# Layer 2 of a two-layer f32 feed-forward kernel: its second block's x asked 8 tiles ahead, its planner given other durations, its last three tiles in another order

## The chip, the core and the metric

One core of one Trainium2 chip runs the whole program. The metric is the device time of one execution in microseconds (us); three runs of the kernel before are given, and one more execution was taken with the hardware profiler.

## What is computed

Linear attention over 8 batches of 8 heads (softmax of q over the head, of k over the sequence, k transposed times v, q times that) gives x of 4608 tokens by 512. Two feed-forward layers follow, each 512 to 2048 to 512, in f32:

```
h = x @ moe_w_in;   g = where(h > 0, h, exp(min(h, 0)) - 1);   x1 = g @ moe_w_out
h = x1 @ moe2_w_in
P = a[0] + a[1]*h + a[2]*h*h + a[3]*h*h*h
Q = 1 + abs(b[0])*abs(h) + abs(b[1])*h*h
out = (P / (Q + 1e-6)) @ moe2_w_out
```

## The kernel before

**Tiles.** A layer has 9 blocks of 512 tokens (j) and 16 slices of 128 of the 2048 inner columns (f). One (layer, j, f) is a tile. Its *in* part, `plan_in`, makes h of 128 x 512 in one PSUM bank (name `ps`, kind `bank`, 4 of them) with 12 matmuls: 4 pieces of x times 3, since each f32 operand is split into a high and a low half of the type that the matmul takes (L781 to L783 hold the three products). Its *out* part, `plan_out`, adds g times w_out into the four accumulators of the block (`acc`), 12 matmuls again (L823). For f = 0 and f = 15 both parts are four operations of 3 matmuls, else one of 12. Layer 2 is 144 tiles of 24 matmuls.

**Between the two parts of a tile of layer 2** stand eleven elementwise operations of 128 x 512, in `plan_rational`: on ACT `pstart` (a[3]*h + a[2], tile `p`, L926), `square` (`s`, L922) and `absb` (|b0 h|, tile `m`, L918), which read the bank; on DVE `pmul` and `pstep` (L944, L947), which read the bank too, the second of them setting it free; on POOL `qsum` (L929); on ACT `root` and `guess` (L932, L935); on DVE `test`, `newton`, `pend` (L938, L941, L951), of which each reads two SBUF tiles; on ACT `hi` and on POOL `lo` (the high and low half of g, L299 and L302; tile `gs` for even f, `g` for odd f). `p` has 3 buffers, and `lo` sets one free; g has 4 in all.

**Order.** All instructions of an engine run in the order in which a planner in the program (`Plan.run`) issues them. It goes through operations with a price each (the number in `ACT(0.8)`, `DVE(0.7)` and so on), takes the one that by these prices can start first, and breaks ties by rank. A price is thus never a time on the chip; it sets only what stands behind what on an engine. PE's order, too, comes out of it.

**x of layer 2.** `plan_x1` loads a block's four pieces of x1 (SP), and makes the high half on ACT and the low half on POOL, with ranks that start 14 tiles ahead of the block, 2 tiles apart.

**Stores.** `plan_store` copies a finished accumulator to `e` on ACT (L863) and sends it off from SP (L867).

Of the kernel before, what the change touches and what calls it, by code (L numbers as in the profile page):

```python
# [13 lines left out]
AF = mybir.ActivationFunctionType  # L14
ALU = mybir.AluOpType
# [19 lines left out]
class Plan:  # L35
# [146 lines left out]
def linear_attention_elu_rational(  # L182
# [46 lines left out]
    late = []  # L229
# [18 lines left out]
    op = plan.op  # L248
# [19 lines left out]
    NTL = 2 * NB * KF
    DMA = 2.2

    def f32_tile(tag, bufs, pool=None):
        return (pool or main).tile([P, TB], F32, tag=tag, name=tag, bufs=bufs)
# [19 lines left out]
    def halves_of(ap):  # L292
        return ap.rearrange("p (h c) -> p h c", h=2)

    def back(ps):
        return ps.rearrange("p (c h) -> p h c", h=2)

    def copy_hi(hi, src):
        nc.scalar.activation(out=hi, in_=src, func=AF.Copy)  # L299
# [454 lines left out]
    in_ops = {}  # L754
# [7 lines left out]
    tiles = [(0, j, f) for part in range(2) for j in range(2) for f in range(*((0, CUT[j]), (CUT[j], KF))[part])]  # L762
# [3 lines left out]
    def step_of(L, j, f):  # L766
        return place[L, j, f]
# [75 lines left out]
    accs = {}  # L843
# [6 lines left out]
    def plan_store(L, j, i, o, r, half):  # L850
        b = {}

        def load(e):
            b["e"] = f32_tile("e", 4)
            nc.sync.dma_start(out=b["e"], in_=part_d[j, i])

        def add(e):
            e = halves_of(b["e"])
            nc.vector.tensor_tensor(out=e, in0=e, in1=back(accs[L, j, i]), op=ALU.add)

        def copy(e):
            b["e"] = f32_tile("e", 4)
            nc.scalar.activation(out=halves_of(b["e"]), in_=back(accs[L, j, i]), func=AF.Copy)  # L863

        def store(e):
            dst = part_d[j, i] if half == 1 else x1_d[j, i] if L == 0 else out[j * TB + i * P:j * TB + (i + 1) * P, :]
            nc.sync.dma_start(out=dst, in_=b["e"])  # L867

        free = [("acc", acc_op[L, j, i])]
        if half == 2:  # L870
            l = op(SP, load, [parts_stored[j, i], in_ops[0, j, KF - 1]], r - 1, take=["e"], extra=DMA)
            o1 = op(DVE(), add, [l, o], r, free=free)
        else:
            l = o1 = op(ACT(), copy, [o], r, take=["e"], free=free)
        o = op(SP, store, [o1], r, extra=DMA, free=[("e", l)])
        if half == 1:
            parts_stored[j, i] = o
        else:
            stored[L, j, i] = o
# [31 lines left out]
    def plan_rational(t):  # L911
        b = {}
        s = step_of(*t)
        gkind = ("gs", "g2")[t[2] % 2]

        def absb(e):
            b["a"] = f32_tile("m", 2)
            nc.scalar.activation(out=b["a"], in_=b["h"], func=AF.Abs, scale=b_sb[:, 0:1])  # L918

        def square(e):  # L920
            b["s"] = f32_tile("s", 3, late[0])
            nc.scalar.activation(out=b["s"], in_=b["h"], func=AF.Square, scale=b_sb[:, 1:2])  # L922

        def pstart(e):
            b["p"] = f32_tile("p", 3, late[0])
            nc.scalar.activation(out=b["p"], in_=b["h"], func=AF.Identity, scale=a_sb[:, 3:4], bias=a_sb[:, 2:3])  # L926

        def qsum(e):
            engine[e].tensor_tensor(out=b["s"], in0=b["s"], in1=b["a"], op=ALU.add)  # L929

        def root(e):
            nc.scalar.activation(out=b["a"], in_=b["s"], func=AF.Abs_reciprocal_sqrt, scale=2.0**-48, bias=qbias)  # L932

        def guess(e):
            nc.scalar.activation(out=b["a"], in_=b["a"], func=AF.Square, scale=2.0**-24)  # L935

        def test(e):
            nc.vector.scalar_tensor_tensor(out=b["s"], in0=b["s"], scalar=1.0 + 1e-6, in1=b["a"], op0=ALU.add, op1=ALU.mult)  # L938

        def newton(e):  # L940
            nc.vector.scalar_tensor_tensor(out=b["a"], in0=b["s"], scalar=-2.0, in1=b["a"], op0=ALU.add, op1=ALU.mult)  # L941

        def pmul(e):
            nc.vector.tensor_tensor(out=b["p"], in0=b["p"], in1=b["h"], op=ALU.mult)  # L944

        def pstep(e):
            nc.vector.scalar_tensor_tensor(out=b["p"], in0=b["p"], scalar=a_sb[:, 1:2], in1=b["h"],  # L947
                                           op0=ALU.add, op1=ALU.mult)

        def pend(e):  # L950
            nc.vector.scalar_tensor_tensor(out=b["p"], in0=b["p"], scalar=a_sb[:, 0:1], in1=b["a"],  # L951
                                           op0=ALU.add, op1=ALU.mult)

        def hi(e):
            if gkind == "gs":
                b["g"] = main.tile([P, 2, TB], F32R, tag="gs", name="gs", bufs=2)
            else:
                b["g"] = late[0].tile([P, 2, TB], F32R, tag="g2", name="g2", bufs=2)
            copy_hi(b["g"][:, 0], b["p"])

        def lo(e):
            sub_lo(e, b["g"][:, 1], b["p"], b["g"][:, 0])

        o = plan_in(t, b)
        p1 = op(ACT(0.8), pstart, [o, late_op], s + 0.5, take=["p"])
        o1 = op(ACT(0.69), square, [p1], s + 0.52, take=["s"])
        o2 = op(ACT(0.69), absb, [o1], s + 0.53, take=["m"])
        p2 = op(DVE(0.7), pmul, [p1], s + 0.6)
        p3 = op(DVE(0.7), pstep, [p2, o2], s + 0.61, free=[("bank", b["h_op"])])
        o3 = op(SOONEST if s >= NTL - 2 else POOL(), qsum, [o2], s + 0.7)  # L970
        o4 = op(ACT(0.72), root, [o3], s + 0.8)
        o5 = op(ACT(), guess, [o4], s + 0.82)
        o6 = op(DVE(1.0), test, [o5], s + 0.9)
        o7 = op(DVE(1.0), newton, [o6], s + 0.91, free=[("s", o1)])
        p4 = op(DVE(1.0), pend, [o7, p3], s + 1.01, free=[("m", o2)])
        g1 = op(ACT(), hi, [p4], s + 1.3, take=[gkind])
        b["g_op"] = op(SOONEST if s >= NTL - 2 else POOL(), lo, [g1], s + 1.4, free=[("p", p1)])
        b["g_free"] = (gkind, g1)
        plan_out(t, b)

# [20 lines left out]
    for n in range(2 * KF):  # L1001
        f, which = divmod(n, 2)
        s = KF + 3 * n
# [7 lines left out]
    late_op = op((("", 0.0),), open_late, at_ops, None)  # L1011

    for f in range(KF):
        for which in range(2):
            b = {}
            r = step_of(0, NB - 1, f) + (0.9, 3.0)[which]
# [7 lines left out]
            l = op(SP, load, [late_op, stored["w", f, which], gone], r, take=["hc"], extra=DMA)  # L1024
# [14 lines left out]
    def plan_x1(j, i):  # L1039
        b = {}  # L1040
        kind = "xs"
        r = step_of(1, j, 0) - 14 + 2 * i

        def load(e):
            b["e"] = f32_tile("e", 4)
            nc.sync.dma_start(out=b["e"], in_=x1_d[j, i])
            x_tile[1, j, i] = main.tile([P, 2, TB], F32R, tag="xs", name="xs", bufs=8)

        def hi(e):
            copy_hi(x_tile[1, j, i][:, 0], b["e"])  # L1050

        def lo(e):
            x = x_tile[1, j, i]
            sub_lo(e, x[:, 1], b["e"], x[:, 0])

        early = in_ops[tiles[max(0, step_of(1, j, 0) - 14)]]
        l = op(SP, load, [late_op, stored[0, j, i], early, last.get("x1")], r, take=["e", kind], extra=DMA)
        last["x1"] = l
        o = op(ACT(), hi, [l], r + 1)
        x_ready[1, j, i] = op(POOL(), lo, [o], r + 1.1, free=[("e", l)])  # L1060
        x_owner[1, j, i] = kind, l
# [7 lines left out]
    with tc.manual_schedule():  # L1069
# [25 lines left out]
        o = op(SP, load_ab, [in_ops[0, 1, 0]], 0.0)  # L1095
        op(ACT(0.2), minus_a, [o, in_ops[0, 2, 0]], 0.0)
        o = op(ACT(0.2), abs_b1, [o, in_ops[0, 2, 0]], 0.0)
        o = op(DVE(0.1), seed_b1, [o], 0.0)
        for _ in range(3):
            o = op(DVE(0.5), heron, [o], 0.0)  # L1100
# [69 lines left out]
```

## Time and profile before

| what | value |
|---|---|
| three runs | 1587.16, 1588.49 (median), 1590.0 us |
| the profiled execution: own time | 1586.46 us |
| its span, first to last instruction | 1584.7 us |
| busy share: PE, DVE, ACT, POOL | 99%, 67%, 66%, 46% |
| granted TensorE clock, mean | 0.999 of full speed |

In the profile PE is TensorE's matmuls, DVE VectorE, ACT ScalarE, POOL GpSimd, SP the engine that issues the DMAs. A time in brackets behind an instruction is how long its engine had stood idle before it, and what ended that. In names, what is written stands left of `<-`, and numbers of buffers are left out.

### The profile page before, as it was taken

The numbers are of one execution on the slowest core, as the hardware profiler recorded it, in microseconds if no ns is written. First come the engines' busy times: TensorE is split into PE (matmuls) and PEld (weight loads), VectorE is DVE, ScalarE is ACT, GpSimd is POOL, SyncE is SP. The second block draws the span as 40 slices with busy tenths as digits, with TensorE's granted clock in tenths as the row PEclk, the third lists the DMA queues.
The fourth block names the chain that finished last, engine by engine and source line by source line (L and its number), as shares of the span: only waits on it lengthen the run. The fifth ranks groups of instructions, "written<-read, shape, count | busy, mean of one in ns | idle before, by whom it ended". The sixth has DMA issues, their size and how long they took to land.

```text
span 1584.7 us, 22781 instructions
## 1 busy us (share of the span) xinstructions
PE 1566.1 (99%) x8344; PEld 1350.2 (85%) x8344; DVE 1056.1 (67%) x1659; ACT 1038.9 (66%) x1825; POOL 727.4 (46%) x529
## 2 busy tenths in 40 slices
PE   8999999999999999999999999999999999999998
PEld 7788888888888888888887888888888888888886
DVE  7998766564656566431227867786877686778776
ACT  6767655554646455444558777777777777777776
POOL 3201223232333232333666666666566657665554
PEclk9999999999999999999999999999999999999999
DMA  9523542332322332101422010101010100100000
GB/s 352 202 85 98 170 145 96 98 117 77 123 92 90 103 114 85 50 5 44 137 87 80 0 54 1 54 1 54 1 53 1 42 13 21 34 7 21 0 28 27
DMA packets 48784, 113.31 MB, mean 72 GB/s; under 512 B 5664, under 2 KB 5664, under 8 KB 46624
## 3 DMA queue, kind: packets, MB, share of 16 engines
q1 hardware_dynamic: 48672, 111.85, 20.6%
q8 instruction: 66, 1.08, 0.3%
q14 instruction: 46, 0.38, 0.1%
HBM read 82.47 MB, written 29.36 MB: 71 GB/s over the span
## 4 chain that ended last, share of the span: by engine, by line
PE 91%; ACT 3%; DVE 2%; issue 2%; POOL 1%; DMA 0%; POOLq 0%; SPq 0%; DVEq 0%; ACTq 0%
PE acc L823 44%; PE ps L781 15%; PE ps L783 15%; PE ps L782 15%; PE ps L637 1%; PE ps L510 1%; ACT p L926 1%; POOL gs L302 1%; ACT s L922 1%; ACT m L932 0%; ACT m L935 0%; DMA e<-in_q_dram 0%; DVE s L938 0%; PE ps L276 0%; DVE m L941 0%
## 5 line engine op out<-in xcount | busy, mean ns | idle before, releaser
L781 PE MATMUL ps<-xs,w_in 128*128 128x512 f32 x1152 | 437.7, 380 | 3.3 <-DVE p L947 3.0
L782 PE MATMUL ps<-xs,w_in 128*128 128x512 f32 x1152 | 436.7, 379 | 0.0
L783 PE MATMUL ps<-xs,w_in 128*128 128x512 f32 x1152 | 436.6, 379 | 0.0
L823 PE MATMUL acc<-gs,w_out 128*128 128x512 f32 x1728 | 403.5, 381 | 2.0 <-DVE w_out L302 1.5
L823 PEld LDWEIGHTS acc<-gs,w_out 128*128 128x128 f32 x1728 | 324.2, 189 | 54.0 <-ACT gs L299 3.5
L302 POOL TENSOR_TENSOR gs<-m,gs 128x512 fp32r<-128x512 f32 x96 | 124.6, 1298 | 283.8 <-ACT gs L299 266.0
L781 PEld LDWEIGHTS ps<-xs,w_in 128*128 128x128 f32 x1152 | 217.7, 189 | 36.7 <-issue 4.4
L782 PEld LDWEIGHTS ps<-xs,w_in 128*128 128x128 f32 x1152 | 217.7, 189 | 30.9 <-DVE xs L302 0.2
L783 PEld LDWEIGHTS ps<-xs,w_in 128*128 128x128 f32 x1152 | 217.7, 189 | 30.8
L893 DVE SCALAR_TENSOR_TENSOR m<-m,ps 128x512 f32<-128x512 f32 x144 | 98.4, 683 | 196.1 <-ACT m L890 189.0
L929 POOL TENSOR_TENSOR s<-s,m 128x512 f32<-128x512 f32 x144 | 218.5, 1518 | 16.9 <-ACT m L918 16.9
L302 POOL TENSOR_TENSOR gs<-p,gs 128x512 fp32r<-128x512 f32 x72 | 116.0, 1611 | 231.9 <-issue 193.5
L823 PE MATMUL acc<-w_out,gs 128*128 128x512 f32 x864 | 201.8, 380 | 2.7 <-ACT gs L299 1.6
L823 PE MATMUL acc<-w_out,g 128*128 128x512 f32 x864 | 199.8, 379 | 0.5 <-POOL g L302 0.5
L887 ACT ACTIVATE m<-ps 128x512 f32<-128x512 f32 x144 | 85.9, 597 | 161.5 <-PE ps L783 128.6
L938 DVE SCALAR_TENSOR_TENSOR s<-s,m 128x512 f32<-128x512 f32 x144 | 142.5, 990 | 69.1 <-ACT m L935 69.0
L823 PEld LDWEIGHTS acc<-w_out,gs 128*128 128x128 f32 x864 | 162.4, 189 | 29.0 <-POOL gs L302 4.3
L823 PEld LDWEIGHTS acc<-w_out,g 128*128 128x128 f32 x864 | 163.2, 189 | 24.0 <-POOL g L302 0.9
L926 ACT ACTIVATE p<-ps,a_sb 128x512 f32<-128x512 f32 x144 | 112.2, 779 | 79.7 <-POOL gs L302 73.6
L299 ACT ACTIVATE gs<-m 128x512 fp32r<-128x512 f32 x144 | 90.4, 628 | 99.0 <-PE acc L823 80.5
L947 DVE SCALAR_TENSOR_TENSOR p<-p,a_sb,ps 128x512 f32<-128x512 f32 x144 | 107.4, 746 | 57.4 <-ACT m L918 57.3
L951 DVE SCALAR_TENSOR_TENSOR p<-p,a_sb,m 128x512 f32<-128x512 f32 x144 | 136.7, 949 | 2.1
(122 smaller groups left out, 1922.5 us busy)
## 6 DMA issues: line engine op xcount, KB each, us to landing
x<-e SPq DMA_DIRECT2D x36, 256.0 KB, 2.2
e<-x SPq DMA_DIRECT2D x36, 256.0 KB, 3.0
out_dram<-e SPq DMA_DIRECT2D x36, 256.0 KB, 2.0
bits<-in_moe_w_in_dram SPq DMA_DIRECT2D x8, 1024.0 KB, 9.6
bits<-in_moe_w_out_dram SPq DMA_DIRECT2D x8, 1024.0 KB, 11.4
st<-in_moe_w_in_dram SPq DMA_DIRECT2D x16, 512.0 KB, 4.6
w<-st SPq DMA_DIRECT2D x32, 256.0 KB, 2.0
st<-in_moe_w_out_dram SPq DMA_DIRECT2D x16, 512.0 KB, 4.2
```

Of the source, the lines that this page charges most:

```text
L299: nc.scalar.activation(out=hi, in_=src, func=AF.Copy)
L302: engine[e].tensor_tensor(out=lo, in0=src, in1=hi.bitcast(F32), op=ALU.subtract)
L781: nc.tensor.matmul(o, w[:, 0, kk, :], two(x[:, 0]), start=(kk == 0), stop=False)
L782: nc.tensor.matmul(o, w[:, 0, kk, :], two(x[:, 1]), start=False, stop=False)
L783: nc.tensor.matmul(o, w[:, 1, kk, :], two(x[:, 0]), start=False, stop=(kk == KD - 1))
L823: nc.tensor.matmul(turned(o), lhsT, two(rhs), start=(f == f0 and n == 0), stop=(f == f1 and n == 2))
L893: nc.vector.scalar_tensor_tensor(out=b["m"], in0=b["m"], scalar=-1.0, in1=b["h"], op0=ALU.add, op1=ALU.max)
L926: nc.scalar.activation(out=b["p"], in_=b["h"], func=AF.Identity, scale=a_sb[:, 3:4], bias=a_sb[:, 2:3])
L929: engine[e].tensor_tensor(out=b["s"], in0=b["s"], in1=b["a"], op=ALU.add)
L938: nc.vector.scalar_tensor_tensor(out=b["s"], in0=b["s"], scalar=1.0 + 1e-6, in1=b["a"], op0=ALU.add, op1=ALU.mult)
L947: nc.vector.scalar_tensor_tensor(out=b["p"], in0=b["p"], scalar=a_sb[:, 1:2], in1=b["h"], op0=ALU.add, op1=ALU.mult)
L951: nc.vector.scalar_tensor_tensor(out=b["p"], in0=b["p"], scalar=a_sb[:, 0:1], in1=b["a"], op0=ALU.add, op1=ALU.mult)
```

## The change

It moves x of layer 2's second block from 14 to 8 tiles ahead; it gives the planner other prices for layer 2's eleven operations; in the last three tiles `square` and `absb` come ahead of `pstart`, |h| lies in a buffer of kind `e`, and in the last two p lies in one of kind `hc` (free by then) and `lo` is fixed to DVE; and the last accumulator's copy is shared by ACT and DVE.

```diff
@@ plan_store
-            nc.scalar.activation(out=halves_of(b["e"]), in_=back(accs[L, j, i]), func=AF.Copy)
+            half = slice(0, 1 if (L, j, i) == (1, NB - 1, 3) else 2)
+            nc.scalar.activation(out=halves_of(b["e"])[:, half], in_=back(accs[L, j, i])[:, half], func=AF.Copy)
+
+        def rest(e):
+            nc.vector.tensor_scalar(out=halves_of(b["e"])[:, 1], in0=back(accs[L, j, i])[:, 1], scalar1=1.0, scalar2=None,
+                                    op0=ALU.mult)
...
+            if shared:
+                o1 = op(DVE(0.4), rest, [l], r, free=free)
@@ plan_rational
+        ending = s >= NTL - 3
+        akind = "e" if ending else "m"
+        pkind = "hc" if s >= NTL - 2 else "p"
...
-        p1 = op(ACT(0.8), pstart, [o, late_op], s + 0.5, take=["p"])
-        o1 = op(ACT(0.69), square, [p1], s + 0.52, take=["s"])
-        o2 = op(ACT(0.69), absb, [o1], s + 0.53, take=["m"])
-        p2 = op(DVE(0.7), pmul, [p1], s + 0.6)
-        p3 = op(DVE(0.7), pstep, [p2, o2], s + 0.61, free=[("bank", b["h_op"])])
...
+        if ending:
+            o1 = op(ACT(0.61), square, [o], s + 0.5, take=["s"])
+            o2 = op(ACT(0.61), absb, [o1], s + 0.51, take=[akind])
+            p1 = op(ACT(0.72), pstart, [o2], s + 0.53, take=[pkind])
+        else:
+            p1 = op(ACT(0.72), pstart, [o, late_op], s + 0.5, take=["p"])
+            o1 = op(ACT(0.61), square, [p1], s + 0.52, take=["s"])
+            o2 = op(ACT(0.61), absb, [o1], s + 0.53, take=["m"])
+        p2 = op(DVE(0.62), pmul, [p1], s + 0.6)
+        p3 = op(DVE(0.68), pstep, [p2, o2], s + 0.61, free=[("bank", b["h_op"])])
+        o3 = op(SOONEST if s >= NTL - 2 else POOL(1.45), qsum, [o2], s + 0.7)
...
-        b["g_op"] = op(SOONEST if s >= NTL - 2 else POOL(), lo, [g1], s + 1.4, free=[("p", p1)])
+        b["g_op"] = op(DVE(0.7) if s >= NTL - 2 else POOL(1.45), lo, [g1], s + 1.4, free=[(pkind, p1)])
@@ plan_x1
-        r = step_of(1, j, 0) - 14 + 2 * i
+        ahead = 14 if j != 1 else 8
+        r = step_of(1, j, 0) - ahead + 2 * i
```

**POOL, first block of layer 2.** Here `s<-s,m` is `qsum`, `gs` and `g2` the `lo` of an even and an odd tile, and `xs` a piece of the second block's x. Before:

```order
L929 TENSOR_TENSOR s_7761<-s_7761,m_7782 128x512
L302 TENSOR_TENSOR g2_7794<-p_7673,g2_7794 128x512
L302 TENSOR_TENSOR xs_7705<-e_7703,xs_7705 128x512
L929 TENSOR_TENSOR s_7802<-s_7802,m_7820 128x512
L302 TENSOR_TENSOR xs_7730<-e_7728,xs_7730 128x512
L302 TENSOR_TENSOR xs_7839<-e_7837,xs_7839 128x512
L302 TENSOR_TENSOR gs_7879<-p_7731,gs_7879 128x512
L929 TENSOR_TENSOR s_7853<-s_7853,m_7881 128x512
L302 TENSOR_TENSOR xs_7863<-e_7861,xs_7863 128x512
L302 TENSOR_TENSOR g2_7908<-p_7787,g2_7908 128x512
```

The same place in the changed kernel (its L940 is the old L929):

```order
L302 TENSOR_TENSOR g2_7780<-p_7673,g2_7780 128x512
L940 TENSOR_TENSOR s_7729<-s_7729,m_7760 128x512
L940 TENSOR_TENSOR s_7785<-s_7785,m_7793 128x512
L302 TENSOR_TENSOR gs_7862<-p_7719,gs_7862 128x512
L940 TENSOR_TENSOR s_7812<-s_7812,m_7864 128x512
L302 TENSOR_TENSOR g2_7869<-p_7783,g2_7869 128x512
L940 TENSOR_TENSOR s_7887<-s_7887,m_7892 128x512
L302 TENSOR_TENSOR xs_7911<-e_7909,xs_7911 128x512
L302 TENSOR_TENSOR gs_7941<-p_7810,gs_7941 128x512
L940 TENSOR_TENSOR s_7915<-s_7915,m_7943 128x512
L302 TENSOR_TENSOR xs_7936<-e_7934,xs_7936 128x512
L302 TENSOR_TENSOR g2_7968<-p_7872,g2_7968 128x512
```

The four pieces no longer stand among the first tiles' `lo`; they come some four tiles later.

**PE, from the sixth to the seventh block of layer 2.** `w_in` and `w_out` name the weights of two slices: 6987 are f = 0 and 1 and 7114 are f = 4 and 5 of the in part, 7752 (7751 in the changed kernel) are f = 14 and 15 of the out part, `g2` there being f = 15. Before, the last product of the in tile f = 4 of the new block, then out of f = 15 of the old one, then the next in tile:

```order
L781 MATMUL ps_11966<-xs_11273,w_in_7114 128x512
L782 MATMUL ps_11966<-xs_11273,w_in_7114 128x512
L783 MATMUL ps_11966<-xs_11273,w_in_7114 128x512
L823 MATMUL acc_11334<-w_out_7752,g2_11962 128x512 x3
L823 MATMUL acc_11342<-w_out_7752,g2_11962 128x512 x3
L781 MATMUL ps_12004<-xs_11201,w_in_7114 128x512
L782 MATMUL ps_12004<-xs_11201,w_in_7114 128x512
```

In the changed kernel, out of f = 14, the last quarter of the in tile f = 0 of the new block, out of f = 15, and the in tile f = 1:

```order
L823 MATMUL acc_11346<-w_out_7751,gs_11875 128x512 x3
L823 MATMUL acc_11375<-w_out_7751,gs_11875 128x512 x3
L823 MATMUL acc_11407<-w_out_7751,gs_11875 128x512 x3
L823 MATMUL acc_11412<-w_out_7751,gs_11875 128x512 x3
L781 MATMUL ps_11832<-xs_11344,w_in_6987 128x512
L782 MATMUL ps_11832<-xs_11344,w_in_6987 128x512
L783 MATMUL ps_11832<-xs_11344,w_in_6987 128x512
L823 MATMUL acc_11346<-w_out_7751,g2_11895 128x512 x3
L781 MATMUL ps_11906<-xs_11255,w_in_6987 128x512
L782 MATMUL ps_11906<-xs_11255,w_in_6987 128x512
```

The old block's f = 15 was used with four more tiles of the new block already made on PE; now it is used with one. Ahead of this point eight quarters of in tiles alternate with eight whole out tiles, behind it eight whole in tiles with eight quarters of out tiles. The order is the same at the ends of the third to the eighth block; at the ends of the first and the second, f = 15 stands behind in tile f = 3 and f = 1.

**ACT, the end of the program.** Before, the last two tiles' operations (`m` is |h|, later the reciprocal):

```order
L926 ACTIVATE p_13939<-ps_13847,a_sb_137 128x512
L922 ACTIVATE s_13942<-ps_13847,b_sb_138 128x512
L299 ACTIVATE g2_13945<-p_13869 128x512
L932 ACTIVATE m_13921<-s_13911,qbias_140 128x512
L918 ACTIVATE m_13949<-ps_13847,b_sb_138 128x512
L935 ACTIVATE m_13921<-m_13921 128x512
L932 ACTIVATE m_13949<-s_13942,qbias_140 128x512
```

In the changed kernel (L933 square, L929 |h|, L937 p):

```order
L299 ACTIVATE gs_13914<-p_13801 128x512
L933 ACTIVATE s_13934<-ps_13836,b_sb_138 128x512
L929 ACTIVATE e_13937<-ps_13836,b_sb_138 128x512
L937 ACTIVATE hc_13940<-ps_13836,a_sb_137 128x512
L299 ACTIVATE gs_13943<-hc_13886 128x512
L943 ACTIVATE e_13937<-s_13934,qbias_140 128x512
```

The last tile's square and |h| stand ahead of its p, which no longer takes one of the three `p` buffers.

## Rows read from the trace of the kernel before

**Rows 1.** The page, busy time, share of the span and instructions of each engine.

```profile
PE 1566.1 (99%) x8344; PEld 1350.2 (85%) x8344; DVE 1056.1 (67%) x1659; ACT 1038.9 (66%) x1825; POOL 727.4 (46%) x529
```

**Rows 2.** PE's waits in layer 2: total us, times, longest us.

```profile
PE ps L781 <- DVE p L947: 3.0, 2, 2.8
```

**Rows 3.** Timeline of PE: start us, us, instruction, idle time before it.

```profile
855.12 0.45 PE L781 MATMUL ps<-xs,w_in 128*128 128x512 f32 x1 [2.84 <-DVE p L947]
...
1570.14 2.43 PE L823 MATMUL acc<-w_out,g 128*128 128x512 f32 x10 [0.46 <-POOL g L302]
...
1574.16 0.70 PE L823 MATMUL acc<-w_out,gs 128*128 128x512 f32 x2 [1.59 <-ACT gs L299]
...
1575.89 2.43 PE L823 MATMUL acc<-w_out,gs 128*128 128x512 f32 x10 [1.03 <-POOL gs L302]
```

**Rows 4.** Windows, one block long: us, busy us and instructions by engine, clock, DMA.

```profile
1157.00:1240.00 83.00, 83.00 (x385) 72.42 (x384) 62.15 (x81) 62.50 (x105) 52.84 (x37) 1.00 0.08 26
```

**Rows 5.** Chain of waits: one out tile, and the same PE piece in three blocks.

```profile
1181.07 3.88 PE acc L823 x18
...
1264.16 3.88 PE acc L823 x18
...
1347.26 3.88 PE acc L823 x18
...
1442.02 2.59 PE acc L823 x12
```

**Rows 6.** Timeline of POOL inside the seventh block.

```profile
1357.36 1.28 POOL L929 TENSOR_TENSOR s<-s,m 128x512 f32<-128x512 f32 x1
...
1365.68 1.28 POOL L302 TENSOR_TENSOR g<-p,g 128x512 fp32r<-128x512 f32 x1 [0.34 <-POOL s L929]
...
1371.53 1.67 POOL L302 TENSOR_TENSOR gs<-p,gs 128x512 fp32r<-128x512 f32 x1 [3.33 <-issue]
...
1381.10 1.67 POOL L302 TENSOR_TENSOR gs<-p,gs 128x512 fp32r<-128x512 f32 x1 [3.34 <-issue]
...
1390.66 1.67 POOL L302 TENSOR_TENSOR gs<-p,gs 128x512 fp32r<-128x512 f32 x1 [3.33 <-issue]
```

**Rows 7.** Timeline of ACT there, one odd tile's p and g.

```profile
1354.11 0.78 ACT L926 ACTIVATE p<-ps,a_sb 128x512 f32<-128x512 f32 x1 [1.27 <-POOL gs L302]
...
1364.93 0.62 ACT L299 ACTIVATE g<-p 128x512 fp32r<-128x512 f32 x1
```

**Rows 8.** Chain of waits: ACT's time for a copy and for a high half.

```profile
1510.03 0.49 ACT e L863
1510.52 0.52 ACT g L299
```

**Rows 9.** Timeline of POOL ahead of the stall at 855.

```profile
848.68 1.74 POOL L302 TENSOR_TENSOR xs<-e,xs 128x512 fp32r<-128x512 f32 x1
850.75 1.35 POOL L302 TENSOR_TENSOR xs<-e,xs 128x512 fp32r<-128x512 f32 x1 [0.33 <-ACT xs L299]
```

**Rows 10.** Timeline of DVE ahead of that stall, and two operations at 1325 alone.

```profile
850.89 1.76 DVE L938 SCALAR_TENSOR_TENSOR s<-s,m 128x512 f32<-128x512 f32 x1
852.68 1.64 DVE L941 SCALAR_TENSOR_TENSOR m<-s,m 128x512 f32<-128x512 f32 x1
854.24 0.73 DVE L947 SCALAR_TENSOR_TENSOR p<-p,a_sb,ps 128x512 f32<-128x512 f32 x1
...
1325.80 0.68 DVE L938 SCALAR_TENSOR_TENSOR s<-s,m 128x512 f32<-128x512 f32 x1
1326.52 0.69 DVE L941 SCALAR_TENSOR_TENSOR m<-s,m 128x512 f32<-128x512 f32 x1
```

**Rows 11.** Timeline of all engines at the end.

```profile
1566.81 0.78 ACT L926 ACTIVATE p<-ps,a_sb 128x512 f32<-128x512 f32 x1 [1.25 <-POOL gs L302]
...
1574.25 1.58 POOL L302 TENSOR_TENSOR gs<-p,gs 128x512 fp32r<-128x512 f32 x1 [2.92 <-ACT gs L299]
...
1577.14 0.69 DVE L302 TENSOR_TENSOR g<-p,g 128x512 fp32r<-128x512 f32 x1 [0.76 <-ACT g L299]
```

More of the change, by code (lines that the diff above doesn't have):

```diff
@@ L873, in plan_store @@
         else:
-            l = o1 = op(ACT(), copy, [o], r, take=["e"], free=free)
-        o = op(SP, store, [o1], r, extra=DMA, free=[("e", l)])
+            shared = (L, j, i) == (1, NB - 1, 3)
+            l = o1 = op(ACT(0.4 if shared else 0.62), copy, [o], r, take=["e"], free=[] if shared else free)
+            if shared:
+                o1 = op(DVE(0.4), rest, [l], r, free=free)
+        o = op(SP, store, [o1, l], r, extra=DMA, free=[("e", l)])
         if half == 1:
@@ L914, in plan_rational @@
         gkind = ("gs", "g2")[t[2] % 2]
+        ending = s >= NTL - 3
+        akind = "e" if ending else "m"
+        pkind = "hc" if s >= NTL - 2 else "p"
         def absb(e):
-            b["a"] = f32_tile("m", 2)
+            b["a"] = f32_tile(akind, 4 if ending else 2)
             nc.scalar.activation(out=b["a"], in_=b["h"], func=AF.Abs, scale=b_sb[:, 0:1])
@@ L924, in pstart @@
         def pstart(e):
-            b["p"] = f32_tile("p", 3, late[0])
+            b["p"] = f32_tile(pkind, 3, late[0])
             nc.scalar.activation(out=b["p"], in_=b["h"], func=AF.Identity, scale=a_sb[:, 3:4], bias=a_sb[:, 2:3])
@@ L964, in plan_rational @@
         o = plan_in(t, b)
-        p1 = op(ACT(0.8), pstart, [o, late_op], s + 0.5, take=["p"])
-        o1 = op(ACT(0.69), square, [p1], s + 0.52, take=["s"])
-        o2 = op(ACT(0.69), absb, [o1], s + 0.53, take=["m"])
-        p2 = op(DVE(0.7), pmul, [p1], s + 0.6)
-        p3 = op(DVE(0.7), pstep, [p2, o2], s + 0.61, free=[("bank", b["h_op"])])
[L970 to L976, printed above, removed]
-        b["g_op"] = op(SOONEST if s >= NTL - 2 else POOL(), lo, [g1], s + 1.4, free=[("p", p1)])
+        if ending:
[9 more added lines that the diff above has]
+        o3 = op(SOONEST if s >= NTL - 2 else POOL(1.45), qsum, [o2], s + 0.7)
+        o4 = op(ACT(0.65), root, [o3], s + 0.8)
+        o5 = op(ACT(0.55), guess, [o4], s + 0.82)
+        o6 = op(DVE(0.9), test, [o5], s + 0.9)
+        o7 = op(DVE(0.75), newton, [o6], s + 0.91, free=[("s", o1)])
+        p4 = op(DVE(0.85), pend, [o7, p3], s + 1.01, free=[(akind, o2)])
+        g1 = op(ACT(0.55), hi, [p4], s + 1.3, take=[gkind])
+        b["g_op"] = op(DVE(0.7) if s >= NTL - 2 else POOL(1.45), lo, [g1], s + 1.4, free=[(pkind, p1)])
         b["g_free"] = (gkind, g1)
@@ L1054, in lo @@
             sub_lo(e, x[:, 1], b["e"], x[:, 0])
-        early = in_ops[tiles[max(0, step_of(1, j, 0) - 14)]]
+        early = in_ops[tiles[max(0, step_of(1, j, 0) - ahead)]]
         l = op(SP, load, [late_op, stored[0, j, i], early, last.get("x1")], r, take=["e", kind], extra=DMA)
```

## Prediction

> **What bounds the kernel now.** I read the busy shares first [rows 1]: PE is busy 99% of the span. All that a new order can remove is PE's idle time, so the waits of PE came next. In layer 2 they are few: 3.0 us for a bank that `pstep` sets free, nearly all of it one stall of 2.84 us before an in tile of the first block [rows 2, 3], and three at the very end, 0.46 + 1.59 + 1.03 = 3.1 us, for the g of the last three tiles [rows 3]. 6.1 us is all that the change can take from PE's waits here. Then the windows: in a whole block of layer 2 PE has no idle time, 83.00 us of 83, with ACT and DVE at 62 [rows 4]. The same piece of PE's work comes back after 83.1 us, block by block (1264.16 - 1181.07, 1347.26 - 1264.16) [rows 5]. That looks like ample room on the other engines. It is not, and the timeline of POOL shows why: inside a block `lo` of the even tiles starts at 1371.53, 1381.10 and 1390.66, so the eleven operations give two tiles per 9.56 us, 4.78 us a tile [rows 6], though PE would wait for none of them. They are a chain over three engines, and the p of a tile waits for the `lo` of the tile three before it, since `p` has three buffers: ACT idles 1.27 us for that [rows 7]. PE needs 83.1 / 16 = 5.19 us a tile. So the chain has only 0.4 us of room a tile, 6.6 us a block, whatever the busy shares say, and of that four copies and four high halves of x take 4 x 0.49 + 4 x 0.52 = 4.0 us of ACT [rows 8].
>
> **The change, part by part.** The sum is made against the profiled execution's own 1586.46 us, which is 1.76 us more than its span and 2.03 us under the median of the runs, 1588.49.
>
> *x of the second block.* The stall at 855.12 ended with the `pstep` at 854.24, which stood behind a `test` of 1.76 us and a `newton` of 1.64 on DVE, where the same two take 0.68 and 0.69 elsewhere [rows 10]. In those microseconds POOL ran pieces of x, 1.74 and 1.35 us [rows 9]; a DVE operation with two SBUF inputs and a POOL operation do not run side by side here. The order shows the four pieces gone from that place: -3.0. No operation is gone, though: four high halves (2.1 us of ACT by [rows 8]) and four low halves come some four tiles later, where the chain has 0.4 us a tile of room. I take the 2.1 back, so -0.9; the ends are -3.0 (all of it fits there) and +0.5 (all of the stall comes back, with one DVE operation delayed by half of what it was at 852).
>
> *The prices.* This is the large part, though it moves no operation from one engine to another. From the third block's end to the eighth's, PE now uses the old block's last tile right behind the in tile f = 0 of the new one. PE goes in order, so it makes no further h until the g of tile 15 is there; by then everything older is done, and the eleven operations have one tile to start from. The chain runs dry and must fill again, once a block; before, four more tiles of h lay ready at that point. Its cycle, from one such point to the next, is worked out thus:
> - tile 1's h comes 3.24 us after tile 0's: a quarter out tile and a whole in tile, 15 of the 12 matmuls that take 2.59 us [rows 5];
> - an odd tile needs 12.85 us from its p to the end of its `lo`: p at 1354.11, its square sum at 1357.36, its high half at 1364.93, its low half from 1365.68 to 1366.96 [rows 6, 7];
> - seven more pairs to tile 15, 7 x 9.56 = 66.9 us;
> - together 83.0 us, and 87.0 with the 4.0 us of copies and high halves, if none of them falls into a moment when ACT idles anyway.
>
> While the chain fills, ACT idles often, so I take half of the 4.0: 85.0 us, against 83.1 that PE needs. The longer one sets the pace: +1.9 us a cycle, with 0 and +3.9 as the ends. I count five cycles for blocks three to seven (first block = zero), one for the second (two), and half a one for block one, whose chain does not run dry altogether: 6.5 x 1.9 = +12.4. The waits show at two places: an in tile about f = 8 that waits for a bank, since the eight in tiles in a row are asked for at 3.24 us each and made at 4.78, and the out tile 14 or 15 that waits for `lo`. Nothing else covers them: PE has no other work that it could do first, its order being fixed.
>
> Beside this stands a rule of the Trainium skill. The row is that `test` takes 0.68 us in one place and 1.76 in another [rows 10]; the prices put 0.9 on it everywhere. The page "SBUF — State Buffer", section "Who interferes with whom", says that of a DVE and a GpSimd instruction that need the shared pair of ports the one that issues second waits out the whole of the other. By that rule, and the trace agrees, a mean price holds for no order but the one in which it was measured. With it the refilling stretch, where POOL has x's low halves between its own work, would be dearer than my half: the 1610 of the heavier rival below, where the sum by the rows comes to 1597.
>
> *The last three tiles.* The last p waited 1.25 us for POOL's `lo` [rows 11] and now has a buffer of its own. `lo` of the last but one took 1.58 us on POOL where the last, on DVE, took 0.69 [rows 11]: 0.9. Square and |h| ahead of p let `qsum` start one ACT operation earlier, about 0.7. These 2.85 us lie one behind the other on the path to the end, against 3.1 of stalls: -2.9. The ends are -3.1, and +0.8 if the last block, which now also starts from a dry chain, is late by a cycle's +3.9 against which the 3.1 is won.
>
> *The shared copy.* ACT's half, then DVE's half, which waits for it, then the store: two short operations in place of one of about 0.6 us. I put +0.1, between -0.3 (both at once) and +0.3; the last store alone stands behind it.
>
> Sum: -0.9 + 12.4 - 2.9 + 0.1 = **+8.7 us**. The profiled execution would come to 1595.2, and the runs to 1588.49 + 8.7 = 1597.2.
>
> **The rivals.**
> - *Faster.* The copies and high halves all fall into ACT's idle moments while the chain fills. Then its cycle is 83.0, PE's 83.1 goes on setting the pace, and only the gains stay: -0.9 - 2.9 + 0.1 = -3.7, 1584.8. It decides at the 4.0 us: with 0.1 of it on the cycle, this is over. For it speaks that ACT is busy 62.5 of 83 [rows 4]; against it that ACT's work and idle time lie inside a chain, where an operation put in between delays the next one. 8 in 100.
> - *About the same.* 0.2 to 1.0 of the 4.0 us counts: 6.5 x 0.1 to 0.9 us are lost and 3.7 won, 1585.4 to 1590.7. 9 in 100.
> - *Heavier.* All 4.0 us count, or POOL's low halves hold up DVE as at 850 to 854 [rows 9, 10], where two operations lost a microsecond each; four pieces at one such loss each cost the same 4 us. A cycle loses 3.9: 6.5 x 3.9 - 3.7 = +21.7, 1610. For it: pieces, copies and the refilling fall into the same stretch. 11 in 100. The page named above speaks for this one.
> - *The change does not do what it says.* The first block's stall stays, because the pieces only move it, and the end's stalls stay, because the last block starts dry: +12.4 + 0.1, 1601. Both depend on tiles that are delayed by the same pace. 7 in 100.
>
> **How the numbers follow.** The forecast has 65 in 100. Differences under 0.2% (3.2 us) a measurement of this kernel can't tell from none. Slower by more are the forecast, the heavier case and the change that fails, 83 in 100; about the same 9, faster 8. The forecast's own range goes from 1 to 3.2 us a cycle: 6.5 to 20.8, less 3.7, 1591 to 1605.5. To leave out no more than 2 in 10 it is carried on into half of the middle case and some way towards the heavier one: 1589 to 1607.
>
> **What would show it.** In the changed kernel's profile: PE's stall at 855 gone or under 1 us, with smaller ones before in tiles of the first block; in each later block one to three stalls that come back with the block, on L781 released by DVE's `pstep` and on L823 released by POOL's `lo`, 1 to 3 us together; the same PE piece back after 84.5 to 86 us in place of 83.1; ACT, DVE and POOL idle together for some us right ahead of the in tile f = 1; the three stalls at the end gone or under 0.5 us. If a block still takes 83.1 us, the account of the dry chain is wrong and the kernel is faster. If a block takes 87 or more, the copies or the port weigh in full. If the first or last block holds the loss, I misjudged the moved pieces or the end.

## The result and the profile after

The changed kernel takes 1600.59 us (median of five runs, 1599.64 to 1601.36) against 1587.16 for the kernel before on the same chip (five runs, 1585.08 to 1590.0): ratio 1.0084, 95% interval 1.0072 to 1.0096, 13.4 us slower. The forecast was slower by 8.7 us, the range 1589 to 1607. The profiled execution took 1599.64 us with a span of 1597.9; against before's 1586.46 that is +13.2.

The page's busy line, to compare with [rows 1]:

```profile
PE 1568.2 (98%) x8344; PEld 1349.2 (84%) x8344; DVE 1070.0 (67%) x1661; ACT 1041.2 (65%) x1825; POOL 720.9 (45%) x528
```

PE's waits in layer 2 (total us, times, longest us), to compare with [rows 2, 3]:

```profile
PE ps L781 <- DVE p L958: 14.7, 11, 2.2
PE acc L823 <- POOL gs L302: 2.6, 6, 1.0
PE acc L823 <- POOL g L302: 0.2, 1, 0.2
```

17.5 us of waits stand where 6.1 stood. The timeline of PE shows where (start us, us, instruction, idle time before it):

```profile
840.71 0.45 PE L781 MATMUL ps<-xs,w_in 128*128 128x512 f32 x1 [0.76 <-DVE p L958]
...
902.06 0.92 PE L823 MATMUL acc<-w_out,gs 128*128 128x512 f32 x3 [1.03 <-POOL gs L302]
...
934.53 0.45 PE L781 MATMUL ps<-xs,w_in 128*128 128x512 f32 x1 [2.20 <-DVE p L958]
...
1019.17 0.45 PE L781 MATMUL ps<-xs,w_in 128*128 128x512 f32 x1 [1.65 <-DVE p L958]
...
1024.02 0.45 PE L781 MATMUL ps<-xs,w_in 128*128 128x512 f32 x1 [1.37 <-DVE p L958]
...
1252.41 0.92 PE L823 MATMUL acc<-w_out,gs 128*128 128x512 f32 x3 [0.30 <-POOL gs L302]
...
1280.34 0.45 PE L781 MATMUL ps<-xs,w_in 128*128 128x512 f32 x1 [1.54 <-DVE p L958]
...
1337.62 0.91 PE L823 MATMUL acc<-w_out,gs 128*128 128x512 f32 x3 [0.28 <-POOL gs L302]
...
1365.55 0.45 PE L781 MATMUL ps<-xs,w_in 128*128 128x512 f32 x1 [1.54 <-DVE p L958]
```

The stall of 2.84 us at 855 is gone, but the first block has four smaller ones (two of them shown) that add up to 2.8. From the third block's end on, two stalls come back with every block, 0.3 us on L823 and 1.54 on L781, and with them the block: 1337.62 - 1252.41 = 85.21 us, where the same piece came back after 83.1 [rows 5]. The three stalls at the end [rows 3] are gone altogether. The last stall of the program is 0.28 us at 1508.05: the last block starts from the same order of PE at a block's end, but has no further block's x to make, and it has no stall at all.

That the chain has nothing to start from at a block's end is seen on ACT and POOL, 3 to 6 us behind the out tile at 1252.41:

```profile
1255.53 0.78 ACT L937 ACTIVATE p<-ps,a_sb 128x512 f32<-128x512 f32 x1 [1.90 <-PE ps L783]
1258.40 1.28 POOL L940 TENSOR_TENSOR s<-s,m 128x512 f32<-128x512 f32 x1 [3.36 <-ACT m L929]
```

The p waits for PE's h. From 910 to 1555 us twelve p of the changed kernel do so, 13.7 us in all; in the kernel before none does there, its p wait for POOL's `lo`. Such waits are no loss by themselves (in the run with ACT's prices back, below, twenty p wait 35.9 us so); what counts is how long the chain then takes to fill. ACT, DVE and POOL are idle together for 0.5 us only, though, where the prediction expected some us. A window of one such cycle (us, busy us and instructions of PE, PEld, DVE, ACT, POOL, clock, DMA):

```profile
1252.41:1337.62 85.21, 83.39 (x384) 72.42 (x384) 64.73 (x81) 62.58 (x104) 52.72 (x36) 1.00 0.08 26
```

PE is busy 83.39 us for work that took 83.1 before: a matmul behind a stall stands there with 0.45 us, and starting again costs some 0.15 us a stall (0.29 us for two, an estimate). Behind the longest stall lies one more cost. Windows of PE's clock there:

```profile
934.00:935.00 1.00, 0.47 (x2) 0.47 (x3) 0.38 (x1) 1.00 (x3) 1.00 (x2) 1.00 0.00 0
935.00:936.00 1.00, 1.00 (x5) 0.88 (x5) 0.69 (x1) 0.86 (x3) 1.00 (x1) 0.85 0.00 0
936.00:937.00 1.00, 1.00 (x4) 0.72 (x3) 0.00 (x0) 1.00 (x3) 1.00 (x2) 0.50 0.00 0
937.00:938.00 1.00, 1.00 (x4) 0.81 (x3) 0.87 (x2) 1.00 (x3) 0.64 (x2) 0.50 0.00 0
938.00:939.00 1.00, 1.00 (x3) 0.79 (x3) 1.00 (x2) 0.84 (x2) 1.00 (x1) 0.50 0.00 0
939.00:940.00 1.00, 1.00 (x6) 0.82 (x5) 1.00 (x2) 0.94 (x2) 0.00 (x0) 0.94 0.00 0
```

After 2.20 us without a matmul the granted clock was 0.50 (1.2 GHz) for over 3 us, in which PE's matmuls start 0.43 us apart (936.08, 936.51, 936.94) in place of 0.22: 0.15 + 3 x 0.50 + 0.06 = 1.7 us lost. So the account of the +13.2 is: waits 17.5 - 6.1 = +11.4; the clock +1.7; 13 more stalls to start again from, at 0.15, +1.9; and -2.1, because this execution was that much earlier before layer 2 had begun (the same L781 behind a stall of the first layer stands at 131.05 before and at 128.97 after). Together +12.9. Most of that 2.1 is the clock as well. Windows from 20 to 30 us, the kernel before first:

```profile
20.00:30.00 10.00, 8.76 (x65) 7.30 (x66) 9.07 (x19) 6.27 (x10) 3.43 (x3) 0.83 1.02 413
20.00:30.00 10.00, 9.17 (x73) 7.41 (x74) 9.83 (x16) 6.99 (x13) 4.34 (x3) 1.00 1.02 416
```

The profiled execution of the kernel before lost 10 x 0.17 = 1.7 us of clock there, in a part that the change doesn't touch, and that of the changed kernel none. So between these two executions the clock comes to about nothing, and waits and restarts are what is left, 11.4 + 1.9 = 13.3.

### The profile page after: what moved, and what is told of

Its sections match the earlier page's. It is cut to its first block, busy times and chain, and to the rows that moved or that the text cites. A ratio compares the mean times of both kernels' runs of the same rounds, so it can differ in the third digit from the quotient of the medians.

```text
span 1597.9 us, 22819 instructions
## 1 busy us (share of the span) xinstructions
PE 1568.2 (98%) x8344; PEld 1349.2 (84%) x8344; DVE 1070.0 (67%) x1661; ACT 1041.2 (65%) x1825; POOL 720.9 (45%) x528
## 4 chain that ended last, share of the span: by engine, by line
PE 56%; ACT 16%; DVE 14%; POOL 7%; issue 5%; DMA 1%; SPq 0%; POOLq 0%; DVEq 0%; ACTq 0%
PE acc L823 27%; PE ps L781 9%; PE ps L783 9%; PE ps L782 9%; POOL gs L302 5%; DVE s L949 3%; ACT p L937 3%; ACT s L933 3%; DVE p L962 3%; ACT m L943 3%; DVE m L952 2%; DVE p L955 2%; ACT m L929 2%; ACT gs L299 2%; ACT g L299 2%
## 5 line engine op out<-in xcount | busy, mean ns | idle before, releaser
L781 PE MATMUL ps<-xs,w_in 128*128 128x512 f32 x1152 | 439.0, 381 | 15.0 <-DVE p L958 14.7
L823 PE MATMUL acc<-gs,w_out 128*128 128x512 f32 x1728 | 403.4, 381 | 1.8 <-DVE w_out L302 1.3
L823 PEld LDWEIGHTS acc<-gs,w_out 128*128 128x128 f32 x1728 | 324.1, 189 | 53.8 <-ACT gs L299 3.5
L781 PEld LDWEIGHTS ps<-xs,w_in 128*128 128x128 f32 x1152 | 217.9, 189 | 52.0 <-issue 18.3
L940 POOL TENSOR_TENSOR s<-s,m 128x512 f32<-128x512 f32 x141 | 206.2, 1463 | 65.2 <-ACT m L929 65.2
L823 PE MATMUL acc<-w_out,gs 128*128 128x512 f32 x864 | 203.6, 380 | 2.6 <-POOL gs L302 2.6
L823 PE MATMUL acc<-w_out,g 128*128 128x512 f32 x864 | 202.4, 379 | 0.2 <-POOL g L302 0.2
L823 PEld LDWEIGHTS acc<-w_out,gs 128*128 128x128 f32 x864 | 163.0, 189 | 28.5 <-POOL gs L302 5.2
L823 PEld LDWEIGHTS acc<-w_out,g 128*128 128x128 f32 x864 | 163.3, 189 | 23.8 <-POOL g L302 0.6
L302 POOL TENSOR_TENSOR gs<-p,gs 128x512 fp32r<-128x512 f32 x71 | 112.1, 1578 | 153.6 <-ACT gs L299 116.5
L937 ACT ACTIVATE p<-ps,a_sb 128x512 f32<-128x512 f32 x142 | 110.5, 778 | 75.2 <-POOL gs L302 53.0
L949 DVE SCALAR_TENSOR_TENSOR s<-s,m 128x512 f32<-128x512 f32 x141 | 137.9, 978 | 29.5 <-ACT m L946 27.3
L955 DVE TENSOR_TENSOR p<-p,ps 128x512 f32<-128x512 f32 x142 | 96.8, 682 | 84.8 <-ACT p L937 32.3
```

The lines of the kernel that those rows point to most:

```text
L302: engine[e].tensor_tensor(out=lo, in0=src, in1=hi.bitcast(F32), op=ALU.subtract)
L781: nc.tensor.matmul(o, w[:, 0, kk, :], two(x[:, 0]), start=(kk == 0), stop=False)
L823: nc.tensor.matmul(turned(o), lhsT, two(rhs), start=(f == f0 and n == 0), stop=(f == f1 and n == 2))
```

## Experiments

Theory: the new prices move out of f = 15, the chain of eleven operations runs dry at each block's end, and ACT's copies and high halves prolong its refilling. Rivals: the moved x or the new end has a share; POOL's low halves of x do what I put down to ACT; the order on the other engines does it, not PE's. The ratios below are to the kernel before, with their 95% interval.

### The change taken apart

**Only x of the second block moved** (kernel before, with this):

```diff
-        r = step_of(1, j, 0) - 14 + 2 * i
+        ahead = 14 if j != 1 else 8
+        r = step_of(1, j, 0) - ahead + 2 * i
...
-        early = in_ops[tiles[max(0, step_of(1, j, 0) - 14)]]
+        early = in_ops[tiles[max(0, step_of(1, j, 0) - ahead)]]
```

> The kernel before, with x of the second block 8 tiles ahead and nothing else. By the prediction's term the 3.0 us of stall go and 2.1 us come back later in the block: -0.9 us. In the changed kernel the first block still lost 2.88 us in small stalls, which would fit that. Rival: what the changed kernel lost there came from the new prices, and the move by itself takes nearly the whole stall away, -2.3 to -3.0 us, with no stall over 0.5 us left in the first two blocks.

Measured: 1584.17 us against 1587.10, 0.9981 (0.9971 to 0.9991). Of the first two blocks' stalls one over 0.2 us is left:

```profile
874.61 0.92 PE L823 MATMUL acc<-w_out,gs 128*128 128x512 f32 x3 [0.64 <-POOL gs L302]
```

2.84 us went and 0.64 came, a little over the rival's sign of 0.5. The move alone takes most of the stall away; of the 2.1 us that I had come back, 0.6 did.

**Only the prices** (kernel before, with the numbers of `ACT(0.72)` to `POOL(1.45)` as in the change; `hi` and `lo` have new prices too, so thirteen operations, not eleven).

> The kernel before, with the new prices of the eleven operations and nothing else. If the prices carry the loss, the blocks from the second on lose what they lost in the changed kernel (14.7 us) and a block comes back after about 85.2 us; with the first block's and the end's 3 us each still there this gives +12 to +17 us. Rival: the moved x and the new end have their share in it, and the prices alone cost 6 us or less.

Measured: 1600.76 us, 1.0089 (1.0075 to 1.0103), as much as the whole change. From the second block on its stalls are those of the changed kernel within 0.3 us each, so the prices carry the loss. Two things come beside it. The first block has 1.23 us at 852.80 and three smaller stalls, 2.5 us together, though x is asked 14 tiles ahead: under the new prices the moved x wins nothing. And at the end one stall of 0.69 us is left, where [rows 3] have 3.1, though p, square and |h| stand as before: under the new prices the end is nearly mended without its new order.

**All but the prices** (changed kernel with the old prices), twice:

> The changed kernel with the old prices everywhere (moved x, new end, shared copy). By the prediction's sum the three gains stay and the loss goes: -0.9 - 2.9 + 0.1 = -3.7 us against before. Rival: the end's gain hangs on the new prices, since they also set the order of the last tiles; with the old ones the new end orders p, square and |h| so that tiles wait for each other, and the end loses some us instead of winning 3: +3 to +9 us.

> The changed kernel with the old prices everywhere, a second time, to see where its 7.6 us lie. If they are the end's, PE shows stalls of some 10 us together in the last 40 us of the span and none over 0.7 us before, and a block comes back after 83.1 us. If they are the moved x's or spread over the blocks, the end shows less than 4 us.

Measured: 1594.69 us, 1.0050 (1.0036 to 1.0063), and 1594.95, 1.0051 (1.0031 to 1.0071). The second run's profile gives the place:

```profile
1564.67 0.48 PE L823 MATMUL acc<-w_out,g 128*128 128x512 f32 x1 [2.30 <-ACT g L299]
...
1566.07 1.22 PE L823 MATMUL acc<-w_out,g 128*128 128x512 f32 x2 [0.59 <-POOL g L302]
...
1575.59 1.22 PE L823 MATMUL acc<-w_out,gs 128*128 128x512 f32 x2 [4.88 <-ACT gs L299]
```

With 0.50 more at 1577.30 that is 8.3 us of stalls at the end, where there were 3.1. PE's clock there (windows as above):

```profile
1570.00:1576.00 6.00, 1.12 (x3) 0.42 (x2) 5.72 (x10) 3.03 (x5) 0.34 (x1) 0.50 0.00 0
1576.00:1582.00 6.00, 5.50 (x13) 3.89 (x13) 3.20 (x4) 0.63 (x1) 1.25 (x1) 0.50 0.01 3
```

The clock stays at 0.50 from 1565 to 1582, so PE works at half speed between the stalls and for 4.8 us more behind the last one. So the new end without the new prices does not win 3 us, it loses, and the whole run loses 7.6. The two edits are not additive.

### What prolongs the refilling

**POOL's low halves left out** (changed kernel):

```diff
+            if j > 1:
+                nc.sync.dma_start(out=x[:, 1].bitcast(F32), in_=x1_d[j, i])
+                return
             sub_lo(e, x[:, 1], b["e"], x[:, 0])
```

> The changed kernel; from layer 2's third block on, POOL leaves out the low halves of x: a DMA writes x itself in their place, so those products are not the reference's. All instruction orders stay. The prediction's account: while the chain refills, what prolongs it is ACT's copies and high halves; POOL's low halves stand beside it, the cycle stays at 85.2 us or falls by 0.5 at most, 1596 us or more. Rival: POOL's four low halves, which stand in one unbroken row with its other work right behind each block end, are what makes the cycle longer than PE's 83.1; without them it is 83.1 and the stalls from the third block on go, 1589 to 1591 us.

Measured: 1586.53 us, 0.9996 (0.9986 to 1.0006). 14 us less than the changed kernel, with every order kept, and below even the rival's 1589. PE's waits in layer 2:

```profile
PE ps L781 <- DVE p L958: 3.8, 5, 1.4
PE acc L823 <- POOL gs L302: 1.6, 3, 1.0
```

Of the stalls that came back with each block none over 0.4 us is left; the longest that remains, 1.40 us at 1020.50, belongs to the second block's end. POOL's timelines show what was taken away. First the changed kernel at the start of a block (`xs` the low halves, `s` the `qsum`, `gs` and `g` the `lo`):

```profile
1265.32 1.37 POOL L302 TENSOR_TENSOR xs<-e,xs 128x512 fp32r<-128x512 f32 x1 [1.58 <-ACT xs L299]
1266.65 1.72 POOL L302 TENSOR_TENSOR gs<-p,gs 128x512 fp32r<-128x512 f32 x1
1268.34 1.73 POOL L940 TENSOR_TENSOR s<-s,m 128x512 f32<-128x512 f32 x1
1270.03 1.73 POOL L302 TENSOR_TENSOR xs<-e,xs 128x512 fp32r<-128x512 f32 x1
1271.73 1.27 POOL L302 TENSOR_TENSOR g<-p,g 128x512 fp32r<-128x512 f32 x1
1272.97 1.27 POOL L940 TENSOR_TENSOR s<-s,m 128x512 f32<-128x512 f32 x1
1274.20 3.42 POOL L302 TENSOR_TENSOR xs<-e,xs 128x512 fp32r<-128x512 f32 x2
...
1282.67 1.28 POOL L302 TENSOR_TENSOR g<-p,g 128x512 fp32r<-128x512 f32 x1 [0.36 <-POOL s L940]
```

Then the same place without the low halves:

```profile
1258.48 1.28 POOL L302 TENSOR_TENSOR gs<-p,gs 128x512 fp32r<-128x512 f32 x1 [2.68 <-issue]
1259.73 1.72 POOL L940 TENSOR_TENSOR s<-s,m 128x512 f32<-128x512 f32 x1
1262.80 1.28 POOL L302 TENSOR_TENSOR g<-p,g 128x512 fp32r<-128x512 f32 x1 [1.35 <-issue]
1264.04 1.29 POOL L940 TENSOR_TENSOR s<-s,m 128x512 f32<-128x512 f32 x1
...
1272.64 1.28 POOL L302 TENSOR_TENSOR g<-p,g 128x512 fp32r<-128x512 f32 x1 [0.35 <-POOL s L940]
```

From 1265.32 to 1277.6 POOL has no idle time, in the very stretch in which the chain refills; the four low halves take 1.37 + 1.73 + 3.42 = 6.5 us of it. ACT's p of the first odd tile starts at 1258.82 in the one kernel and at 1250.88 in the other:

```profile
1258.82 0.78 ACT L937 ACTIVATE p<-ps,a_sb 128x512 f32<-128x512 f32 x1 [0.50 <-PE ps L783]
```

```profile
1250.88 0.78 ACT L937 ACTIVATE p<-ps,a_sb 128x512 f32<-128x512 f32 x1 [0.49 <-PE ps L783]
```

To the start of the second odd `lo` it is 1282.67 - 1258.82 = 23.85 us with the low halves and 1272.64 - 1250.88 = 21.76 without. The difference, 2.1 us, is all that a cycle is longer than 83.1. The changed kernel's own last block says the same: it has ACT's four copies to make but no x, and takes 20.82 us for that way (1514.46 to 1535.28).

**ACT's copies and high halves left out** (changed kernel; copies and stores 32 columns wide, high halves from a DMA):

```diff
-                copy_hi(x_tile[1, j, i][:, 0], b["e"])
+            if j < 2:
+                copy_hi(x_tile[1, j, i][:, 0], b["e"])
...
+            if L == 1 and 1 < j < NB - 1:
+                nc.scalar.activation(out=b["e"][:, 0:32], in_=accs[L, j, i][:, 0:32], func=AF.Copy)
...
```

> The changed kernel; from layer 2's third block to the last but one, ACT's copies of the accumulators are 32 columns wide in place of 512, with stores as narrow, and from the third block on x's high half comes from a DMA in place of ACT, so most of the output is left out. All orders stay, POOL's low halves too. The prediction's account: half of these 4.0 us of ACT a block lies on the cycle; without them it falls from 85.2 to 83.1 or 83.2, 1589 to 1591 us. Rival (POOL's low halves): the cycle stays at 84.6 to 85.2, 1596 to 1600 us.

Measured: 1599.24 us, 1.0077 (1.0062 to 1.0092). The stall on L781 stays at 1.68 us, the cycle at 84.81 (1366.26 - 1281.45). The ACT work on which the prediction's term rested, all but the 0.19 us that a narrow copy still takes, is worth 0.4 us a cycle, not 2.

**The low halves on DVE** (changed kernel, `sub_lo("DVE" if j > 1 else e, ...)` for x).

> The changed kernel; from layer 2's third block on, x's low halves run on DVE in place of POOL, at the places that the plan gives them. Orders are otherwise the same, and nothing is left out. If POOL's queue alone is what the refilling chain waits for, the cycle falls to 83.1 to 83.6 us as it did without the low halves, 1587 to 1590 us. Rival: DVE and POOL hold each other up, and an operation of two SBUF inputs delays the refill on either of them; then the cycle stays above 84.6 us, 1596 us or more.

Measured: 1598.22 us, 1.0070 (1.0053 to 1.0086); a cycle of 84.87 us (1364.81 - 1279.94). Moving them off POOL's queue helps by 0.3 us only. So it is not that queue alone. In the timeline of DVE of this kernel, where the low halves take 0.68 us each, `newton` still takes more than twice its time, with POOL's `lo` (1265.82) and `qsum` (1267.26) beside it:

```profile
1265.48 0.68 DVE L949 SCALAR_TENSOR_TENSOR s<-s,m 128x512 f32<-128x512 f32 x1
1266.20 1.66 DVE L952 SCALAR_TENSOR_TENSOR m<-s,m 128x512 f32<-128x512 f32 x1
```

While the chain refills, the engine that gets the low halves has no time to give away four times: POOL had no idle time in the changed kernel, above, and DVE in this run idles once, 0.68 us, from 1261.92 to 1279, while POOL now idles 3.94 us at a time. The Trainium skill, "SBUF — State Buffer", section "Who interferes with whom", has a DVE instruction with two SBUF inputs contend with a GpSimd instruction that reads SBUF; the trace agrees, with 0.69 us [rows 10] and 1.66 for the same operation. How much of the 2.1 us is queue and how much is contention these runs don't tell.

### Which order, and which price

**PE's order by the new prices, the rest by the old** (kernel before; the plan is made with the new prices, PE's order of it is kept, and the plan is made again with the old ones):

```diff
...
+        pe = [o for o in order if o["engines"][0][0] == "PE"]
+        for a, b in zip(pe, pe[1:]):
+            b["follow"].append(a)
...
+        plan.rehearse()
         plan.run()
```

> The kernel before with its old prices for ACT, DVE and POOL, but with PE's order as the new prices make it: the plan is made once with the new prices, PE's order is kept, and the plan is made again with the old ones. If PE's order at the block ends is enough to run the chain dry, a block takes 84.5 to 87 us and the loss is 8 to 20 us. Rival: the loss comes from the order that the new prices make on the other engines; with their old prices a block takes 83.1 us and the time stays within 4 us of before.

Measured: 1609.53 us, 1.0146 (1.0131 to 1.0161), a cycle of 86.44 us (1291.27 - 1204.83). 22.5 us lost is more than the 8 to 20 expected. PE's order is enough; the other engines' new order, made for it, even softens the loss. The counterpart, PE's old order with the new prices elsewhere, was not run.

**ACT's prices back** (changed kernel with `ACT(0.8)`, `(0.69)`, `(0.72)` and the two plain `ACT()`).

> The changed kernel with ACT's old prices (0.8, 0.69, 0.72, 0.62), while DVE's and POOL's stay new. If the order with the dry chain comes from how much dearer DVE and POOL now stand against ACT, ACT's prices alone undo most of it: a block of 83.9 us or less, stalls under 1 us a block, 1584 to 1590 us. Rival: DVE's lower prices make it; then the blocks still lose 2 us each, 1597 us or more.

Measured: 1586.93 us, 1.0001 (0.9992 to 1.0010). A cycle takes 84.25 us (1264.57 - 1180.32), with one stall of 1.13. That lies between the two accounts: ACT's prices alone undo half of a cycle's loss, and with the gains at the start and the end the kernel is as fast as before. The other half needs DVE's or POOL's prices too; which of them was not tried. PE's order lies between as well: counted in the timelines of PE, from the third block's end on out of f = 15 comes with three in tiles of the new block already made here, with one in the changed kernel and with five in the kernel before, at 84.25, 85.21 and 83.1 us a cycle. That number is not all, though: at the first block's end four are made in this run and in the changed kernel, which stalls 2.20 us behind it, where this run has no stall.

### The gains without the loss

**Mixed prices** (changed kernel; old prices but for the last 18 tiles, x of the second block 6 tiles ahead), twice, and the same without the new end and the shared copy:

```diff
+        old = s < NTL - 18
+        c = (0.8, 0.69, 0.7, 0.7, 1.4, 0.72, 0.62, 1.0, 1.0, 1.0) if old else (0.72, 0.61, 0.62, 0.68, 1.45, 0.65, 0.55, 0.9, 0.75, 0.85)
...
-        ahead = 14 if j != 1 else 8
+        ahead = 14 if j != 1 else 6
...
```

> The changed kernel with the old prices for all but the last 18 tiles, the new ones in those, and x of the second block 6 tiles ahead. If the loss lies in the order that the new prices make at the block ends, and the gains at the start and the end are real, the blocks come back after 83.1 us and 4 to 5.5 us are won against before: ratio 0.9965 to 0.9975. If the loss lies in something else (the moved x, the shared copy), it stays, +8 us or more.

> The kernel with mixed prices once more, on the chip of the run without the new end, to compare the two: ratio to before again 0.995 to 0.9975.

> The kernel before with its own order of operations in the last three tiles and its own last copy, but with x of the second block 6 tiles ahead and the new prices in the last 18 tiles. Beside the kernel with mixed prices this takes away only the new end. If the end's gain is the prices', the two are within 2 us of each other, and 4 to 6 us below before. If it is the new order's and the extra buffers', this one shows the three stalls of before at the end and wins only the 3 us of the moved x.

Measured: 1580.13 us, 0.9961 (0.9948 to 0.9975), and 1580.59, 0.9959 (0.9945 to 0.9973); without the new end 1582.01, 0.9970 (0.9960 to 0.9980). PE's waits in layer 2 with mixed prices:

```profile
PE acc L823 <- POOL gs L302: 1.3, 1, 1.3
PE ps L781 <- DVE p L958: 0.2, 1, 0.2
```

This beats both kernels, before by 6 to 7 us, a little more than expected; 4.6 of it are stalls (1.5 us in place of 6.1), and the rest is not accounted for. The new end is worth some 1.4 us in it, but the two intervals overlap; its own stall there is 1.34 us against 2.00 without it, and behind the 2.00 the granted clock was at 0.50 from 1571 to 1574.

## Why the prediction was right, and where by the wrong term

- *What bounds the kernel.* Right: what changed is PE's waits, and they come from a chain that has no room at the block ends, while every busy share stays at two thirds or less.
- *The prices.* The place was right, and the size of a cycle: 85.2 us a cycle against 85.0 forecast, five cycles forecast at 1.9 us of waits, and measured one of 1.9 and four of 1.8. That PE's order is enough to bring the loss is shown by the run with that order alone, which loses 3.3 us a cycle with the old order rules on the other engines; the three orders of PE with one, three and five in tiles made at the block's end fit it. The step that failed is "the 4.0 us of copies and high halves", half of which I took to fall on the cycle. They are worth 0.4 us a cycle. What falls on it is x's four low halves, 2.1 us, without which it is PE's 83.1 again; on DVE in place of POOL they still cost 1.8. I had them only in the heavier rival, at 4 us; the half that I took of the wrong 4 us came to the same sum by chance. The rest of that sum holds: by it the second odd `lo` starts 12.85 - 1.28 + 9.56 = 21.1 us after the first odd p, and the last block, without x, has 20.82. Idle time alone would not have told the two apart: in the changed kernel POOL has none from 1265.32 to 1277.62, but ACT has none from 1258.82 to 1267.85 either, with three of the four copies and two high halves in that stretch.
- *Blocks one and two.* Half a cycle (0.95 us) and one (1.9) were too little: 2.2 us at 934.53, and 1.65 + 1.37 + 0.2 in the second. The first of them also brought the clock down, 1.7 us more, and the 0.15 us of each restart was in no term. Together 1.3 + 1.3 + 1.7 + 1.9 = 6.2 us that the sum lacked, and 0.7 more for x (below); less the 2.1 us of the earlier start of layer 2, mostly the clock in the kernel before, that is 4.8, where 13.2 - 8.7 = 4.5.
- *x of the second block.* The sum had -0.9. By itself the move is -2.9 (0.9981), so most of what I let come back did not. In the changed kernel it is about nothing, 2.8 us of small stalls in place of 3.0, because the prices bring their own stalls to the first block. Right in size to a microsecond there, wrong in reason.
- *The last three tiles.* -2.9 forecast, -3.1 measured: no stall is left. But I gave it to the new order and the buffers; the prices alone take 2.4 of it, and the new end without them costs 5 us of stalls and a slow clock. The fear that the last block starts late from a dry chain did not come true: with no x to make, that block has no stall.
- *The rivals.* "Does not do what it says" was near for the first block alone. "Heavier" had the mechanism, at twice its price. The upper end of "about the same" is 1590.6 by its own sum, not 1590.7.

## What to carry to other kernels

A planner's prices set an order and nothing else: other prices moved PE's use of a block's last tile ahead by four tiles and emptied a chain that had no room, 14 us in 1587; after such a change read first how many tiles lie ready on PE at the block ends. Nor were the new ones the truer durations throughout: on ACT they put 0.72 on `pstart`, which takes 0.78 us in the trace [rows 7], where the old price was 0.8. When a chain of engines refills, several engines can look full in that stretch: leave each one's extra work out in a run of its own and read the cycle, as 4.0 us on ACT cost 0.4 here and four low halves on POOL 2.1. Edits that go through one planner do not add up: try each alone and the pairs.

## What the runs showed of the hardware

That a stall of PE can cost more than its length was not expected. After 2.20 us without a matmul the granted clock was 0.50 for over 3 us, above; single stalls of 2.00 us (without the new end), 2.19 (only the prices), 2.30 (all but the prices) and 3.57 (PE's order alone) brought it down too. It does not follow from the length alone: after the stall of 2.84 us at 855 in the kernel before it stayed at 1.00, and the same three stalls at the end (0.5, 1.6 and 1.0 us) left it at 1.00 in the kernel before (first three lines) and brought it down in the run with only x moved (the others):

```profile
855.00:856.00 1.00, 0.88 (x4) 0.83 (x5) 1.00 (x2) 0.16 (x1) 1.00 (x2) 1.00 0.00 0
1574.00:1575.00 1.00, 0.70 (x2) 0.30 (x2) 0.94 (x2) 0.11 (x1) 0.75 (x1) 1.00 0.00 0
1576.00:1577.00 1.00, 1.00 (x5) 0.89 (x6) 0.38 (x1) 0.53 (x1) 0.00 (x0) 1.00 0.00 0
...
1574.00:1575.00 1.00, 0.52 (x1) 0.50 (x2) 0.97 (x1) 0.00 (x0) 0.42 (x1) 0.58 0.00 0
1575.00:1576.00 1.00, 1.00 (x4) 0.75 (x3) 0.27 (x1) 0.63 (x1) 0.00 (x0) 0.50 0.00 0
1576.00:1577.00 1.00, 1.00 (x4) 0.82 (x3) 0.42 (x1) 0.00 (x0) 0.00 (x0) 0.50 0.00 0
```

Single stalls of up to 1.8 us in layer 2, those that come back with each block among them, left it at 1.00 in all profiled executions. So two executions with the same stalls can differ by a microsecond or two.
